# Two small sums of an attention and expert kernel: an operand laid out in strided pairs, and a ten-column product on another engine

## The chip, the cores and the metric

The kernel runs on one core of a Trainium2 chip. The core has five engines that each work off an instruction list of their own, in order: TensorE (PE in the tables; PEld is its weight load), VectorE (DVE), ScalarE (ACT), GpSimd (POOL) and SyncE (SP, which here only issues transfers). An instruction that has to wait for another engine holds up everything behind it on its own engine. The metric is the device time of one execution in microseconds (us).

## The reference, cut to what matters

Three layers follow one another, all in fp32: attention with 32 packing queries per head, a causal mixture of four expert heads with the two best gates per token, and a gated channel mix.

```python
def sm_attn(qq, kk, vv):                       # q, k, v: (8, 8, 576, 64), p: (8, 8, 32, 64)
    s = scale * qq @ kk.T
    a = exp(s - max(s))
    return a / (sum(a) + 1e-09) @ vv
p_packed = sm_attn(p, k, v)                    # 32 packed tokens per head
x = sm_attn(q, p_packed, p_packed)             # -> (8, 576, 512)

for e in range(4):                             # causal experts, head size 64
    a = exp(s_e - max(s_e))                    # s_e: masked scale * q_e @ k_e.T
    ye = a / (sum(a) + 1e-09) @ v_e @ wo[e]
    out += gate[e] * ye                        # gate: softmax over the two best, else 0

x_prev = out shifted by one token
k = relu((mu_k*x + (1-mu_k)*x_prev) @ w_k)
out = sigmoid((mu_r*x + (1-mu_r)*x_prev) @ w_r) * (k*k @ w_v)
```

The change touches the two places where `sum(a) + 1e-09` is formed: the one of the second attention step (`a / sum` over 32 packed tokens) and the one of the experts, where 1 / (sum + 1e-09) is multiplied by the gate.

## The kernel before, in words

Every fp32 product is made of reduced-precision matmuls on a high and a low part of each operand, so that much of the work beside TensorE is to split tiles: the high part is a cast (names that end in `h`), the low part a difference (names that end in `l`).

The program has two stages. In the first, up to about 465 us, the eight batches (b = 0 to 7) go through attention and experts. Their work is written as small generators: `front(b, g)` is the attention for group g of four heads, `values`, `project`, `soft` and `turn` are the experts' projections, masked exponentials and transposes, `pair_out(b, ep)` is the output of a pair of experts, and `fold` prepares products of weights for the second stage. Tables of hand-written times (`FRONT_T`, `G1_T`, `SOFT_T`, `OUT_LAG`, `FOLD_T`) sort the steps of all generators into one program order; a scheduler in the framework then works out each engine's list from a simulated time and priorities. On the chip the lists are fixed. In the second stage (`kstage` at line 855, `vstage` at line 888, up to 862 us) the channel mix runs as long rows of matmuls.

In `front`, each of the 16 instances (8 batches, 2 groups) holds a tile `st` of 128 partitions by 576 columns, read as 18 blocks of 32. Line 326 sums each block on DVE into `s` (128x18), line 327 adds the epsilon to `s` in place, line 329 takes the reciprocal into `r`, and line 330 multiplies `st` by `r`, on POOL for all batches but the first. Line 323, a little earlier, makes `PWl`, the low part of a PSUM tile. A PSUM tile of that size (`big`) is used in turns by many steps, so the next use waits until the tile is read out.

In `pair_out`, each of the 16 instances (8 batches, 2 pairs of experts) reads `sums`, 5 row tiles by 4 experts for each partition. A pair takes two of every four numbers, so the operand is five pairs at a stride of four; line 546 adds the epsilon and writes ten adjacent numbers `cs`, line 547 takes the reciprocal, line 548 multiplies by the gates `cw` (the tile `gws` in the trace). Then `cx`, a copy of the ten numbers to 640 columns, is made (line 206 on DVE in batches 0 to 6, line 204 on ACT in the last), which TensorE transposes later.

Other names below: line 488 makes the masked scores `ms` of one row tile and their minimum `nb` on DVE, line 492 is their exponential on ACT, line 428 the low parts `l` (of `qs`) and `kl` (of `ks`), which read a `big` tile out of PSUM. `A2h` and `A2l` are the two parts of the attention weights. On POOL, lines 687, 200 and 650 are steps of `fold` and of the splits: `wc` (times `om`), `wh` and `wl`.

Of the kernel before, what the change touches and what calls it, by code (L numbers as in the profile page):

```python
# [9 lines left out]
F32 = mybir.dt.float32  # L10
# [4 lines left out]
ALU = mybir.AluOpType  # L15
AX = mybir.AxisListType
# [3 lines left out]
EPS = 1e-9  # L20
# [37 lines left out]
def kernel(  # L58
# [4 lines left out]
    nc = tc.nc  # L63
    P = 128
# [11 lines left out]
    NCB = S // NPK  # L76
# [17 lines left out]
    def nm(s):  # L94
        uid[0] += 1
        return f"{s}_{uid[0]}"

    def big():
        return psb.tile([P, 1024], F32, tag="big", name=nm("big"))

    def one():
        return pso.tile([P, 512], F32, tag="one", name=nm("one"))
# [32 lines left out]
    def pool(name, bufs, side):  # L135
        cm = tc.tile_pool(name=name, bufs=bufs, side=side, reuse_waits="tile")
        return cm, cm.__enter__()
# [6 lines left out]
    if True:  # L144
# [3 lines left out]
        sm_cm, sm = pool("sm", 4, "left")  # L148
# [53 lines left out]
        def evac(eng, o, x):  # L202
            if eng == "A":
                nc.scalar.copy(o, x)  # L204
            elif eng == "V":
                nc.vector.tensor_copy(o, x)
            else:
                pool_copy(o, x)

        def pool_tt(o, x, y, op):  # L210
            nc.gpsimd.tensor_tensor(o, x, y, op=op)  # L211

        def scores_pair(lhs, rhs):
            ps = big()
            for hf in range(2):
                for jj in range(2):
                    nc.tensor.matmul(
                        ps[64 * jj : 64 * jj + 64, 512 * hf : 512 * hf + SH],
                        lhs[:, 64 * jj : 64 * jj + 64],
                        rhs[:, jj, SH * hf : SH * hf + SH],  # L220
                        start=True, stop=True,
                    )
            return halves(ps)[:, :, :SH]
# [23 lines left out]
        def front(b, g):  # L247
# [33 lines left out]
            for c in range(NT):  # L281
# [10 lines left out]
                op0=ALU.mult, op1=ALU.mult,  # L292
# [7 lines left out]
            s2 = scores_pair(ppT, qT)  # L300
# [3 lines left out]
            st3 = st.rearrange("p (c n) -> p c n", n=NPK)  # L304
# [17 lines left out]
            nc.scalar.copy(bat["PWh"][:, g, :], ps[:, :NQK])  # L322
            nc.vector.tensor_sub(bat["PWl"][:, g, :], ps[:, :NQK], f32(bat["PWh"][:, g, :]))
            yield
            s_ = sm.tile([P, NCB], F32, tag="s2", name=nm("s2"))
            nc.vector.tensor_reduce(s_, st3, op=ALU.add, axis=AX.X)
            nc.vector.tensor_scalar(s_, s_, EPS, None, op0=ALU.add)
            r_ = sm.tile([P, NCB], F32, tag="r2", name=nm("r2"))
            nc.vector.reciprocal(r_, s_)
            small.tensor_tensor(st3, st3, r_.unsqueeze(2).to_broadcast([P, NCB, NPK]), op=ALU.mult)  # L330
            yield
            a2 = fr.tile([P, S], F32, tag="sa", name=nm("a2"), bufs=4)
# [106 lines left out]
        def rowap(base, stride, n, w):  # L439
            return bass.AP(  # L440
                tensor=base.tensor, offset=base.offset, ap=[base.ap[0], [stride, n], [1, w]]
            )
# [4 lines left out]
        def tslice(tb, j, q0, q1):  # L447
            return tb[:, TS * j + q0 : TS * j + q1]
# [90 lines left out]
        def pair_out(b, ep):  # L539

            bat = bats[b]
            vg, cw, sums = bat["vg"], bat["cw"], bat["sums"]
            tabs = [bat.pop(("tb", 2 * ep + ee)) for ee in range(2)]
            cs = sm.tile([P, NT, 2], F32, tag="cs", name=nm("cs"), bufs=2)
            es = slice(2 * ep, 2 * ep + 2)
            nc.vector.tensor_scalar(cs, sums[:, :, es], EPS, None, op0=ALU.add)
            nc.vector.reciprocal(cs, cs)
            nc.vector.tensor_mul(cs, cs, cw[:, :, es])
            cx = ex.tile([P, NT, 2, HD], F32, tag="cx", name=nm("cx"), bufs=1)
            evac(E_CX if b < B - 1 else E_CXL, cx, cs.unsqueeze(3).to_broadcast([P, NT, 2, HD]))  # L550
            avs = []
            for lo, hi in ((QB, S), (0, QB)):
                av = one()
                nj = (hi + P - 1) // P
                for j in range(nj):
                    qo = max(lo, j * P)
                    for ee in range(2):
                        nc.tensor.matmul(  # L558
                            av[64 * ee : 64 * ee + 64, qo - lo : hi - lo],
                            vg[:, j, HD * (2 * ep + ee) : HD * (2 * ep + ee + 1)],  # L560
                            tslice(tabs[ee], j, qo, hi),
                            start=j == 0, stop=j == nj - 1,
                        )
                avs.append((av[:, : hi - lo], lo, hi))
            yield
            cp = big()
            for t in range(NT):
                nc.tensor.transpose(
                    cp[:, t * P : (t + 1) * P], cx[:, t, :, :].rearrange("p e h -> p (e h)"), ident
                )  # L570
            cb = ex.tile([P, 1 + S], F32, tag="cb", name=nm("cb"), bufs=1)
            nc.gpsimd.memset(cb[:, :1], 0.0)
            evac(E_CB, cb[:, 1:], cp[:, TAIL : TAIL + S])
            for ps_, lo, hi in avs:
                nc.vector.tensor_mul(cb[:, 1 + lo : 1 + hi], ps_, cb[:, 1 + lo : 1 + hi])


            dt = ex.tile([P, NS, ST], F32, tag="dt", name=nm("dt"), bufs=1)

            def tokens(o):  # L580
                return rowap(cb[:, o : o + 1], RT, ST, 1).rearrange("p s x -> p (s x)")

            pool_tt(
                dt[:, 0:4:3, :],
                bass.AP(tensor=cb.tensor, offset=cb.offset, ap=[cb.ap[0], [1, 2], [RT, ST]]),
                bass.AP(tensor=cb.tensor, offset=cb[:, 2:].offset, ap=[cb.ap[0], [1, 2], [RT, ST]]),
                ALU.subtract,
            )
            pool_tt(dt[:, 1, :], tokens(1), tokens(2), ALU.add)
            pool_tt(dt[:, 2, :], tokens(2), tokens(1), ALU.subtract)  # L590
            yield
            nc.sync.dma_start(dscr[:, NS * ep : NS * ep + NS, ST * b : ST * b + ST], dt)
            yield
# [334 lines left out]
        for b in range(B):  # L928
            t0 = U * b
            for g in range(NG):  # L930
                add(
                    "front", front(b, g), [t0 + t + g * G1_T[i] for i, t in enumerate(FRONT_T)],
                    None if b else PR0 - 10 * g,
                )
            add("values", values(b), [t0 + t for t in VAL_T])
            for ep in range(2):
                add("project", project(b, ep), [t0 + t for t in PROJ_T[2 * ep : 2 * ep + 2]])
            for e in range(NE):
                for i, group in enumerate(GROUPS):
                    t = t0 + NT * e + SOFT_T[i]  # L940
                    add("soft", call(soft, b, e, group), [t])
                    add("turn", call(turn, b, e, group), [t + TURN_LAG[i]])
            for ep in range(NE // 2):
                add("out", pair_out(b, ep), [t0 + 2 * NT * (ep + 1) + t for t in OUT_LAG])
# [66 lines left out]
```

## Time and profile before

| what | us |
|---|---|
| median of three runs (lowest to highest) | 862.37 (861.75 to 862.72) |
| the profiled execution, from its first to its last instruction | 861.8 |
| PE busy | 809.3 (94%) |
| DVE busy | 580.0 (67%) |
| ACT busy | 390.4 (45%) |
| POOL busy | 387.8 (45%) |

The times are device times of whole runs without a profile. The profile is of one further execution, and its span leaves 0.57 us to the median of the runs; no execution time other than its span is given for it. Busy time does not count waiting inside an engine's queue, but an instruction that is held up after it has started counts as busy for as long as it is held.

### The profile page before, as it was taken

How to read it: one execution, taken by the hardware profiler on the slowest of the kernel's cores; microseconds unless marked ns; L12 is line 12 of the kernel's file. 1: busy time of each engine (PE TensorE's matmuls, PEld its weight loads, DVE VectorE, ACT ScalarE, POOL GpSimd, SP SyncE). 2: the span in 40 equal slices, each digit the busy share in tenths (PEclk: the TensorE clock that was granted, in tenths of full speed). 3: DMA queues.
4: the chain of work that ended last, by engine and by line, in shares of the span. 5: the costliest groups of instructions: out<-in, count | busy, mean ns of one | idle time of the engine just before them, and what ended most of it. 6: DMA issues, size and time to landing. Idle time of an engine off the chain costs nothing. (4 is left out here: it accounts for less than half of the span.)

```text
span 861.8 us, 14939 instructions
## 1 busy us (share of the span) xinstructions
PE 809.3 (94%) x5376; PEld 678.2 (79%) x5376; DVE 580.0 (67%) x1306; ACT 390.4 (45%) x989; POOL 387.8 (45%) x525
## 2 busy tenths in 40 slices
PE   6798999999799899988799998999999999999998
PEld 5485868779587696857667877988888889898896
DVE  3989796888958759899885775545454544544342
ACT  2367667686665767767566562202112122121120
POOL 4577577575765645446451242333413233232230
PEclk9799999999999999999999999999999999999999
DMA  9654553736335255425446984032121231120301
GB/s 312 228 164 154 144 173 112 230 110 165 127 116 161 76 150 162 136 79 161 122 158 219 344 294 170 2 121 74 49 110 37 86 111 49 74 74 4 144 1 74
DMA packets 67290, 113.71 MB, mean 132 GB/s; under 512 B 10128, under 2 KB 46480, under 8 KB 67216
## 3 DMA queue, kind: packets, MB, share of 16 engines
q1 hardware_dynamic: 66640, 112.69, 40.6%
q8 instruction: 43, 0.70, 0.3%
q14 instruction: 31, 0.25, 0.1%
q10 hardware_dynamic: 576, 0.07, 0.1%
HBM read 69.74 MB, written 33.55 MB: 120 GB/s over the span
## 5 line engine op out<-in xcount | busy, mean ns | idle before, releaser
L888 PE MATMUL one<-wvh,kk 128*128 128x512 f32 x576 | 186.1, 391 | 0.4 <-DVE rr L893 0.3
L211 POOL TENSOR_TENSOR kk<-y,kk 128x768 fp32r<-128x768 f32 x48 | 89.7, 1869 | 210.5 <-ACT kk L868 206.8
L888 PEld LDWEIGHTS one<-wvh,kk 128*128 128x128 f32 x576 | 107.8, 188 | 21.7 <-DVE rr L893 1.0
L888 PE MATMUL one<-wvl,kk 128*128 128x512 f32 x288 | 112.5, 391 | 0.0
L492 ACT ACTIVATE ms<-ms,nb 64x64 f32<-64x64 f32 (+4 forms) x160 | 89.5, 559 | 36.1 <-DVE nb L488 34.1
L868 ACT CAST kk<-y 128x768 fp32r<-128x768 f32 x48 | 40.1, 835 | 133.2 <-DVE y L866 96.1
L816 DVE TENSOR_TENSOR y<-big,p 128x256 f32<-128x256 f32 x48 | 20.3, 424 | 117.1 <-POOL kk L211 101.2
L863 ACT COPY p<-big 128x256 f32<-128x256 f32 x48 | 17.9, 372 | 126.4 <-PE big L855 92.2
L204 ACT COPY tb<-one 64x128 f32<-64x128 f32 (+5 forms) x208 | 64.5, 355 | 22.4 <-PE one L522 19.6
L558 PE MATMUL one<-tb,vg 128*64 128x320 f32 (+4 forms) x448 | 59.9, 372 | 5.2 <-DVE nb L488 3.9
L888 PEld LDWEIGHTS one<-wvl,kk 128*128 128x128 f32 x288 | 54.3, 188 | 9.7
L515 PE MATMUL one<-ident,ms 128*128 128x128 f32 x320 | 56.1, 285 | 4.7 <-ACT ms L492 2.2
L558 PEld LDWEIGHTS one<-tb,vg 128*64 128x64 f32 x448 | 37.5, 141 | 26.0 <-DVE nb L488 5.1
L488 DVE CUSTOM_DVE_ANT_0 ms<-one,mstrip 64x64 f32<-64x64 f32 (+3 forms) x128 | 51.5, 420 | 6.8 <-PE one L476 4.6
L515 PEld LDWEIGHTS one<-ident,ms 128*128 128x128 f32 x320 | 39.2, 144 | 15.3 <-issue 3.7
L630 POOL TENSOR_TENSOR dcx<-dcx,dcu 128x256 f32<-128x256 f32 x40 | 31.2, 781 | 43.6 <-DVE dcu L624 34.0
L893 DVE TENSOR_TENSOR rr<-one,rr 128x512 f32<-128x512 f32 x36 | 23.2, 685 | 40.7 <-PE one L888 40.6
L866 DVE SCALAR_TENSOR_TENSOR y<-y 128x768 f32<-128x768 f32 x48 | 47.9, 998 | 1.6
L476 PE MATMUL one<-ks,qs 128*128 128x64 f32 (+3 forms) x128 | 41.6, 350 | 5.8 <-DVE nb L488 2.5
L855 PE MATMUL big<-dh,wk0h 128*128 128x256 f32 x192 | 39.7, 284 | 4.2 <-DVE rr L818 3.8
L200 POOL TENSOR_SCALAR dh<-dl 128x2048 fp32r<-128x2048 f32 x10 | 19.4, 1936 | 48.1 <-DMA dl<-dscr 32.8
L211 POOL TENSOR_TENSOR dt<-cb 128x192 f32<-128x192 f32 (+1 forms) x48 | 32.1, 694 | 19.5 <-issue 16.0
(189 smaller groups left out, 2167.3 us busy)
## 6 DMA issues: line engine op xcount, KB each, us to landing
dl<-dscr SPq DMA_DIRECT2D x10, 1024.0 KB, 6.7
kT<-in_k_dram SPq DMA_DIRECT2D x16, 576.0 KB, 4.3
qT<-in_q_dram SPq DMA_DIRECT2D x16, 576.0 KB, 4.9
rscr<-rr SPq DMA_DIRECT2D x12, 768.0 KB, 4.0
rr<-rscr SPq DMA_DIRECT2D x12, 768.0 KB, 4.3
out_dram<-rr SPq DMA_DIRECT2D x11, 768.0 KB, 3.3
vn<-in_v_dram SPq DMA_DIRECT2D x16, 512.0 KB, 4.6
dscr<-dt SPq DMA_DIRECT2D x16, 384.0 KB, 3.8
```

The lines of the kernel that those rows point to most:

```text
L204: nc.scalar.copy(o, x)
L211: nc.gpsimd.tensor_tensor(o, x, y, op=op)
L476: nc.tensor.matmul(ps[:, po : po + kn], qs[:, i * P : i * P + P], keys[:, ko : ko + kn], start=x == 0, stop=x == 1,)
L488: nc.vector.tensor_tensor_reduce(halves(mv) if last else mv, sv, halves(mk) if last else mk, op0=ALU.add, op1=ALU.min, scale=-SC, scalar=3 ...
L492: nc.scalar.activation(mv, mv, AF.Exp, bias=nb[p0:], scale=-1.0, accum_out=bat["sums"][p0:, i, e : e + 1],)
L515: nc.tensor.transpose(ps[:, at + j * P : at + (j + 1) * P], ms[:, j * P : (j + 1) * P], ident)
L558: nc.tensor.matmul(av[64 * ee : 64 * ee + 64, qo - lo : hi - lo], vg[:, j, HD * (2 * ep + ee) : HD * (2 * ep + ee + 1)], tslice(tabs[ee], ...
L630: nc.gpsimd.tensor_add(f32(t["x"]), f32(t["x"]), f32(t["u"]))
L855: nc.tensor.matmul(ps[:, o : o + EB], wpart("k0" if f < 4 else "k1", s, wx, t)[:, f % 4 * P : f % 4 * P + P], dx[:, NS * t + s, :], start= ...
L866: nc.vector.scalar_tensor_tensor(y, y, 0.0, y, op0=ALU.max, op1=ALU.mult)
L868: nc.scalar.copy(kk[:, 0], y)
L888: nc.tensor.matmul(ps, kk[:, a, x, t0 : t0 + P], wres["v"][b][:, f, :], start=n == 0, stop=n == 3 * NFT - 1,)
```

## The change

In `front`, the 18 block sums are written to a tile of 9 by 4 numbers, of which the first two of each four are used. The epsilon is then added from this strided operand into the 18 adjacent numbers of `r`, and the reciprocal is taken in `r` in place. The sums' tile has two buffers in place of four, with as many bytes in all. In `pair_out`, the product of `cs` and the gates moves from DVE to POOL.

```diff
-            s_ = sm.tile([P, NCB], F32, tag="s2", name=nm("s2"))
-            nc.vector.tensor_reduce(s_, st3, op=ALU.add, axis=AX.X)
-            nc.vector.tensor_scalar(s_, s_, EPS, None, op0=ALU.add)
+            s_ = sm.tile([P, NCB // 2, 4], F32, tag="s2", name=nm("s2"), bufs=2)[:, :, :2]
+            nc.vector.tensor_reduce(
+                s_, st3.rearrange("p (a b) n -> p a b n", b=2), op=ALU.add, axis=AX.X
+            )
             r_ = sm.tile([P, NCB], F32, tag="r2", name=nm("r2"))
-            nc.vector.reciprocal(r_, s_)
+            nc.vector.tensor_scalar(r_.rearrange("p (a b) -> p a b", b=2), s_, EPS, None, op0=ALU.add)
+            nc.vector.reciprocal(r_, r_)
             small.tensor_tensor(st3, st3, r_.unsqueeze(2).to_broadcast([P, NCB, NPK]), op=ALU.mult)
...
             nc.vector.tensor_scalar(cs, sums[:, :, es], EPS, None, op0=ALU.add)
             nc.vector.reciprocal(cs, cs)
-            nc.vector.tensor_mul(cs, cs, cw[:, :, es])
+            nc.gpsimd.tensor_tensor(cs, cs, cw[:, :, es], op=ALU.mult)
```

All lines below the first hunk stand two lines lower in the changed kernel: its line 330 adds the epsilon, 331 is the reciprocal, 332 the product with `st`, and 548, 549 and 550 are the former 546, 547 and 548. Each engine's list also changes elsewhere. Three places show how. The number behind a name tells one tile from another of the same kind.

Place A is DVE's list in batch 3, where the first pair's `cs` (`cs_3269`) is due while masks of later row tiles are made (ISA is the masked minimum of line 488, now 490). Before:

```order
L488 ISA ms_122,nb_689_3245<-one_3240,mstrip 128x192
L488 ISA nb_689_3245 128x1
L488 ISA ms_123,nb_690_3248<-one_3240,mstrip 128x320
L488 ISA nb_690_3248 128x1
L548 TENSOR_TENSOR cs_3269<-cs_3269,gws_2813 128x10
L323 TENSOR_TENSOR PWl_2413<-big_3143,PWh_2412 128x772
L488 ISA ms_124,nb_692_3257<-big_3252,mstrip 128x576
L488 ISA nb_692_3257 128x1
L206 COPY cx_3273<-cs_3269 128x640
```

Now, the same place on DVE, from the reciprocal's successor on:

```order
L490 ISA ms_122,nb_689_3245<-one_3240,mstrip 128x192
L490 ISA nb_689_3245 128x1
L490 ISA ms_123,nb_690_3248<-one_3240,mstrip 128x320
L490 ISA nb_690_3248 128x1
L490 ISA ms_124,nb_692_3257<-big_3252,mstrip 128x576
L490 ISA nb_692_3257 128x1
L323 TENSOR_TENSOR PWl_2413<-big_3143,PWh_2412 128x772
L206 COPY tb_3047<-one_3265 64x64
L326 TENSOR_REDUCE s_673_3184<-st_3067 128x9x2
L262 TENSOR_REDUCE mx_700_3296<-big_3291 128x1
L330 TENSOR_SCALAR r_674_3186<-s_673_3184 128x18
L206 COPY cx_3273<-cs_3269 128x640
```

And POOL's list there, now with the product between two of its long operations:

```order
L718 TENSOR_TENSOR oo_2745<-oo_2745 128x256
L200 TENSOR_SCALAR A2h_2410<-a_681_3213 128x576
L550 TENSOR_TENSOR cs_3269<-cs_3269,gws_2813 128x10
L689 TENSOR_SCALAR wc_3101<-wc_3101,om 128x256 x4
L337 TENSOR_TENSOR A2l_2411<-a_681_3213,A2h_2410 128x576
L332 TENSOR_TENSOR st_3067<-st_3067,r_674_3186 128x576
```

DVE's product is gone from between the masks, the low part `PWl` has changed places with the mask of 576 columns, and the copy `cx` has moved back by three instructions that stand behind `PWl`.

Place B is the second pair of batch 4. On DVE before, the copy stood behind the low part `l`:

```order
L546 TENSOR_SCALAR cs_4480<-sums_3598 128x10
L547 RECIPROCAL cs_4480<-cs_4480 128x10
L548 TENSOR_TENSOR cs_4480<-cs_4480,gws_3568 128x10
L428 TENSOR_TENSOR l_4199<-big_4186,qs_118 128x576
L206 COPY cx_4484<-cs_4480 128x640
L428 TENSOR_TENSOR kl_120<-big_4213,ks_4226 64x576 x2
```

Now `l` stands ahead of the sums, and on DVE nothing lies between the reciprocal and the copy:

```order
L430 TENSOR_TENSOR l_4199<-big_4186,qs_118 128x576
L548 TENSOR_SCALAR cs_4480<-sums_3598 128x10
L549 RECIPROCAL cs_4480<-cs_4480 128x10
L206 COPY cx_4484<-cs_4480 128x640
L430 TENSOR_TENSOR kl_120<-big_4213,ks_4226 64x576 x2
```

On POOL the product now stands behind eight instructions that split weights and queries:

```order
L200 TENSOR_SCALAR qs_118<-qs_118 64x576
L200 TENSOR_SCALAR wh_3857<-wc_3856 128x256 x4
L652 TENSOR_TENSOR wl_3858<-wc_3856,wh_3857 128x256 x2
L461 MEMSET sums_5003 128x20
L550 TENSOR_TENSOR cs_4480<-cs_4480,gws_3568 128x10
L652 TENSOR_TENSOR wl_3858<-wc_3856,wh_3857 128x256 x2
```

The copy has to wait for the product, so it and `kl` behind it now hang on POOL's list.

Place C is the second pair of batch 2. On DVE before:

```order
L548 TENSOR_TENSOR cs_2970<-cs_2970,gws_2058 128x10
L206 COPY cx_2974<-cs_2970 128x640
L428 TENSOR_TENSOR l_2689<-big_2676,qs_118 128x576
L428 TENSOR_TENSOR kl_120<-big_2703,ks_2716 64x576 x2
L644 SCALAR_TENSOR_TENSOR wc_3101<-dcq_3109,dcx_3106 128x256
```

Now, with two steps of `fold` (`wc`, `dcx`) ahead of `kl`:

```order
L549 RECIPROCAL cs_2970<-cs_2970 128x10
L430 TENSOR_TENSOR l_2689<-big_2676,qs_118 128x576
L646 SCALAR_TENSOR_TENSOR wc_3101<-dcq_3109,dcx_3106 128x256
L206 COPY cx_2974<-cs_2970 128x640
L620 SCALAR_TENSOR_TENSOR dcx_3152<-raw_3150,dce_3153 128x256
L430 TENSOR_TENSOR kl_120<-big_2703,ks_2716 64x576 x2
```

On POOL the product stands behind all four `wl`:

```order
L200 TENSOR_SCALAR wh_2348<-wc_2347 128x256 x4
L652 TENSOR_TENSOR wl_2349<-wc_2347,wh_2348 128x256 x3
L461 MEMSET sums_3598 128x20
L652 TENSOR_TENSOR wl_2349<-wc_2347,wh_2348 128x256
L550 TENSOR_TENSOR cs_2970<-cs_2970,gws_2058 128x10
```

The copy has moved from the place right behind the product to one behind `l` and `wc`, and `kl` from the next place but one to one behind `dcx`.

## Rows read from the trace of the kernel before

**Rows 1.** Windows: stretch, length, busy PE PEld DVE ACT POOL, PEclk, DMA share, GB/s.

```profile
0.00:470.00 470.00, 426.00 (x3142) 339.97 (x3144) 384.28 (x1037) 302.85 (x863) 273.35 (x463) 0.96 0.51 156
530.00:862.00 332.00, 327.69 (x1950) 291.79 (x1948) 155.48 (x228) 55.78 (x93) 96.82 (x52) 1.00 0.19 68
```

**Rows 2.** Instructions of tile cs: min/median/max ns, first and last start us.

```profile
L546 DVE TENSOR_SCALAR cs<-sums x16: 151/164/167, 74.2 to 458.1; 128x10 f32<-128x10 f32 x16
L548 DVE TENSOR_TENSOR cs<-cs,gws x16: 157/240/3573, 79.4 to 458.6; 128x10 f32<-128x10 f32 x16
L206 DVE COPY cx<-cs x14: 476/492/968, 81.7 to 404.7; 128x640 f32<-128x640 f32 x14
L204 ACT COPY cx<-cs x2: 709/718/726, 435.4 to 461.2; 128x640 f32<-128x640 f32 x2
```

**Rows 3.** Instructions of line 327, the epsilon of the block sums.

```profile
L327 DVE TENSOR_SCALAR s<-s x16: 134/386/2346, 25.5 to 389.2; 128x18 f32<-128x18 f32 x16
```

**Rows 4.** Timeline of DVE from 229 us: start, duration, instruction, [idle before <-releaser].

```profile
229.47 3.57 DVE L548 TENSOR_TENSOR cs<-cs,gws 128x10 f32<-128x10 f32 x1
232.96 0.95 DVE L323 TENSOR_TENSOR PWl<-big,PWh 128x772 fp32r<-128x772 f32 x1
```

**Rows 5.** Timeline of POOL over the same stretch.

```profile
229.14 0.95 POOL L687 TENSOR_SCALAR wc<-wc,om 128x256 f32<-128x256 f32 x2
...
231.60 1.41 POOL L335 TENSOR_TENSOR A2l<-a,A2h 128x576 fp32r<-128x576 f32 x1
```

**Rows 6.** Timeline of PE behind it.

```profile
234.06 1.40 PE L217 MATMUL big<-kT,pT 128*64 128x288 f32 x6 [3.47 <-DVE PWl L323]
```

**Rows 7.** Timeline of DVE from 284 us.

```profile
284.50 3.39 DVE L548 TENSOR_TENSOR cs<-cs,gws 128x10 f32<-128x10 f32 x1
287.81 0.74 DVE L488 CUSTOM_DVE_ANT_0 ms<-big,mstrip 128x576 f32<-128x576 f32 x1
```

**Rows 8.** Timeline of PE there.

```profile
288.62 0.87 PE L217 MATMUL big<-kT,pT 128*64 128x288 f32 x4 [2.69 <-DVE nb L488]
```

**Rows 9.** Windows around and behind the two waits, columns as in rows 1.

```profile
225.00:245.00 20.00, 16.29 (x105) 11.25 (x106) 14.92 (x36) 13.51 (x40) 13.09 (x23) 0.91 0.19 63
280.00:300.00 20.00, 17.31 (x116) 11.55 (x115) 14.76 (x36) 14.09 (x42) 13.69 (x23) 0.91 0.25 81
290.00:292.00 2.00, 2.00 (x9) 1.23 (x9) 1.51 (x4) 0.26 (x1) 0.00 (x0) 0.50 0.04 6
```

**Rows 10.** Timeline of DVE in batch 0's first pair.

```profile
74.98 0.66 DVE L327 TENSOR_SCALAR s<-s 128x18 f32<-128x18 f32 x1
```

**Rows 11.** Timeline of PE there.

```profile
76.70 1.54 PE L217 MATMUL big<-kT,pT 128*64 128x288 f32 x8 [0.83 <-DVE nb L488]
```

**Rows 12.** Instructions of line 330, the same product on both engines.

```profile
L330 POOL TENSOR_TENSOR st<-st,r x14: 1152/1161/1186, 72.9 to 392.3; 128x576 f32<-128x576 f32 x14
L330 DVE TENSOR_TENSOR st<-st,r x2: 759/872/986, 26.1 to 36.1; 128x576 f32<-128x576 f32 x2
```

**Rows 13.** Timeline of DVE in batch 4's second pair.

```profile
305.02 0.22 DVE L547 RECIPROCAL cs<-cs 128x10 f32<-128x10 f32 x1
...
308.46 1.52 DVE L428 TENSOR_TENSOR kl<-big,ks 64x576 fp32r<-64x576 f32 x2 [1.40 <-ACT ks L426]
```

**Rows 14.** Timeline of POOL there.

```profile
307.71 2.81 POOL L650 TENSOR_TENSOR wl<-wc,wh 128x256 fp32r<-128x256 f32 x4
```

**Rows 15.** Timeline of PE there.

```profile
310.83 0.42 PE L413 MATMUL big<-A2h,PWh 128*128 128x288 f32 x2
```

**Rows 16.** Timeline of DVE in batch 2's second pair.

```profile
197.75 1.52 DVE L428 TENSOR_TENSOR kl<-big,ks 64x576 fp32r<-64x576 f32 x2 [0.94 <-ACT ks L426]
...
199.77 0.78 DVE L618 SCALAR_TENSOR_TENSOR dcx<-raw,dce 128x256 int32<-128x256 int32 x1
```

**Rows 17.** Timeline of POOL there.

```profile
197.07 1.44 POOL L650 TENSOR_TENSOR wl<-wc,wh 128x256 fp32r<-128x256 f32 x2
```

**Rows 18.** Timeline of PE there.

```profile
200.00 0.43 PE L413 MATMUL big<-A2h,PWh 128*128 128x288 f32 x2
```

## The prediction, made before the changed kernel had run

> **What bounds the kernel now.** I read the windows by stage first. In the second stage PE is busy for 327.69 of 332 us at the full granted clock; the change has no instruction there. In the first 470 us PE is busy for 426.00, so 44 us are PE's waits, and DVE is the next busiest engine with 384 us [rows 1]. A gain must come out of waits of PE for DVE in the first stage; time taken from DVE where PE does not wait is worth nothing.
>
> Next I read the groups of the two places. They hold one odd thing. Line 548, a product of ten columns, takes between 0.16 and 3.57 us; line 327, an addition on 18 columns, between 0.13 and 2.35. Line 546, an addition on the same ten columns whose operand lies in strided pairs, never leaves 0.151 to 0.167 [rows 2, 3]. The reader is to see the spread: so small an instruction is not busy for 3 us, it is held. The timelines of DVE and POOL show by what: at 229.47 the product starts while POOL runs its operations from 229.14 back to back, and it ends at 233.04, when the last of six, `A2l`, ends (231.60 + 1.41) [rows 4, 5]. To add up the held time of 32 instances would give no price. Last I read PE's timeline: which of the holds does PE wait for?
>
> Two large ones. After 230.59 PE waits 3.47 us, until `PWl` is there, which stands directly behind the product at 229.47 [rows 4, 6]. After 285.93 it waits 2.69 us for the mask behind the product at 284.50, which is held 3.39 us [rows 7, 8]. A smaller one: the addition at 74.98 is held for 0.66 us and the mask behind it ends a PE wait of 0.83 [rows 10, 11]. I take the other holds as covered: behind no other long one did I find a wait of PE that it ended.
>
> **What each wait costs.** The two large ones cost more than themselves. [...] 20 x 0.09 = 1.8 us of full-speed work each, if all of it lay on PE's path. [...]
>
> **The change part by part.**
>
> *The product leaves DVE (16 times).* At place A, batch 3, DVE comes past the product's old place at 229.55. Now the 576-column mask (0.74, and 0.08 to read its minimum) and then `PWl` (0.95) follow [rows 4, 7]: 229.55 + 0.82 + 0.95 = 231.3. `PWl` was ready at 233.91 before (232.96 + 0.95), PE's matmul began 0.15 behind it, so it begins at about 231.45 in place of 234.06: 2.6 gained. In batch 4 the mask follows the reciprocal directly, so it ends at 284.50 + 0.82 = 285.3, ahead of 285.93, where PE runs out of work: I take the whole 2.7. With the clock's 2 x 1.8 = 3.6 that is 8.9.
>
> *The addition in strided pairs (16 times).* If the form is what spares line 546, line 327's median of 0.39 goes to about 0.16. On the path stands only batch 0's: 0.66 - 0.16 = 0.5. If the form does nothing this is 0. The block sum writes 9x2 numbers in place of 18; no row of before shows that form, and I take no difference: the count of numbers is the same, and at 0.2 us each way in 16 places off the path it would still be nothing. Two buffers for four: the tile is read once, right behind its writing, in the same list, so nothing waits for it.
>
> Full gain: 2.6 + 2.7 + 3.6 + 0.5 = 9.4.
>
> *The product arrives on POOL.* POOL took 1.16 us for a product of 576 columns where DVE takes 0.76 to 0.99 [rows 12]. No row shows ten columns there. It is not below the 0.16 that DVE needs at least [rows 2] and not above 1.16; I take 0.3, nearer to the lower end, as ten columns are a sixtieth of 576. [...]
>
> *What queues behind it.* The price is POOL's list. The copy `cx` on DVE now waits for a product that stands in its turn on POOL, and everything behind the copy on DVE waits too. In the first pairs of batches 3 and 4 the copy stands behind `PWl` and the masks, so POOL has time. In the second pairs it does not.
> - Place B, batch 4. Before, POOL had done `wh`, `qs` and a memset by 307.71 and then four `wl`, 0.70 each (2.81) [rows 14]. Now two of them stand ahead: 307.71 + 1.40 + 0.3 = 309.4, which is 4.2 us after the reciprocal (305.02 + 0.22) [rows 13]. The copy takes 0.49 [rows 2], `kl` 1.52: 311.4. Before, `kl` ended at 309.98 and PE read the next tile of that kind at 310.83 [rows 13, 15]: 0.85 of slack, so 0.6 late.
> - Place C, batch 2. The four `wl` end at 198.51 [rows 17], the product at 198.8, the copy at 199.3, then `dcx` 0.78 and `kl` 1.52: 201.6, against 199.27 before and PE's next use at 200.00 [rows 16, 18]: 1.6 late, or 0.8 if `dcx` is not ready in time to matter.
> I take 0.6 + 1.2 = 1.8 of new waits. In the last batch ACT makes the copies, the last at 461.2, 2.6 behind the last product [rows 2]; that time covers the move.
>
> **The sum.** I keep half of the clock's 3.6, since PE will still stand still near these places for a while and the new waits may bring falls of their own: 9.4 - 1.8 - 1.8 = 5.8. The profiled execution's span is 861.8, 0.57 below the median of the runs, and I make the sum on the median: 862.4 - 5.8 = 856.6. The bounds of the terms: all of the gain and no new wait, 853.0; no clock back and the product at 1.16 in both second pairs (0.9 more each), 862.4 - 9.4 + 3.6 + 1.8 + 1.8 = 860.2.
>
> **The rivals.**
> - *Only one of the large waits goes.* For it: in batch 4 I know that the mask is early, but not that PE's next operand is; every list has changed. Then 2.7 + 1.8 of the gain is lost: 9.4 - 4.5 - 1.8 = 3.1, so 859.3.
> - *Nothing changes.* The hold is not the product's alone: any instruction of DVE that contends with POOL's burst is held in its place, and the copy `cx` is one that varies (0.476 to 0.968 [rows 2]). If the copy, behind the product on POOL, meets the next burst, the wait moves and 862.4 stands, within 1.7. Against it: the copy's worst was half a microsecond. [...]
> - *Slower: DVE waits for POOL in the second pairs.* Each second pair has the product 4 us or so behind its reciprocal where POOL is in a split of weights, and DVE, in order, stands still. If three such places cost PE what the largest wait cost before, 3.4 us each and 1.8 for the clock, the price is 15.6 and the time 862.4 - 9.4 + 15.6 = 868.6. It decides from 9.4 us of new waits on. Against it: batches 2 and 4, worked out above, come to 0.6 and 1.6.
> - *The strided form does not help.* Both large waits hang on the product, so the time would be 857.1, inside the forecast's own range.
>
> **How the numbers follow.** 0.2% of the time, 1.7 us, is about what a measurement of this kernel can tell from no change. Forecast 0.55 (its own range 853 to 860.2); one wait only 0.15 (859.3, part of it within the bound: 0.02); nothing changes 0.17, of which 0.03 falls on faster and 0.02 on slower; slower 0.13 with a mild form (864 to 866) as likely as the full one. Faster: 0.55 + 0.13 + 0.03 = 0.71; same: 0.02 + 0.12 = 0.14; slower: 0.02 + 0.13 = 0.15. A range of 852.5 to 863.5 leaves out about 0.05 below and 0.13 above.
>
> **What would show it right or wrong.** On DVE no addition of the block sums above 0.2 us; if their spread stays, the form is not the reason that line 546 is free. No PE wait of 2 us or more for `PWl` in batch 3 and for a mask in batch 4, and the windows' clock there above 0.91. The ten-column product on POOL at about 0.3. New: DVE idle ahead of the copy `cx` with POOL as releaser, some 4 us in the second pairs of batches 2 and 4, and PE waits of 0.5 to 1.6 us for `kl` there. The forecast is wrong if these waits of DVE are as long in most batches and PE waits behind them, or if PE's waits in batches 3 and 4 stay with another releaser.

## The result and the profile after

The changed kernel takes 849.06 us (847.99 to 850.12, 4 runs) against 862.55 us (861.75 to 863.12, 4 runs) of the kernel before on the same chip: a ratio of 0.9847, with a 95% interval of 0.9831 to 0.9864. It is 13.5 us faster; 5.8 were forecast, and the time lies below the range of 852.5 to 863.5. The profiled execution has a span of 848.0 us, 13.8 below that of before.

The windows by stage of the changed kernel, columns as in [rows 1], and the stretches around the two places of [rows 9]:

```profile
0.00:470.00 470.00, 434.07 (x3216) 346.57 (x3217) 378.32 (x1030) 308.13 (x869) 280.25 (x483) 0.99 0.54 164
225.00:245.00 20.00, 19.78 (x144) 15.05 (x144) 15.10 (x45) 16.49 (x51) 17.00 (x31) 1.00 0.35 98
280.00:300.00 20.00, 18.84 (x152) 16.22 (x149) 10.42 (x30) 14.82 (x44) 13.35 (x26) 1.00 0.41 119
```

In the same 470 us PE is busy 8 us longer, and the trace has 74 matmuls more. At both places the granted clock is now 1.00 over the 20 us, where it had a mean of 0.91.

The instructions of tile `cs` and of the new line 330 (the block sums' epsilon), min/median/max in ns:

```profile
L548 DVE TENSOR_SCALAR cs<-sums x16: 121/164/167, 73.3 to 446.1; 128x10 f32<-128x10 f32 x16
L550 POOL TENSOR_TENSOR cs<-cs,gws x16: 196/210/386, 75.9 to 447.0; 128x10 f32<-128x10 f32 x16
L206 DVE COPY cx<-cs x14: 429/846/3667, 78.8 to 395.5; 128x640 f32<-128x640 f32 x14
```
```profile
L330 DVE TENSOR_SCALAR r<-s x16: 127/160/172, 24.4 to 379.2; 128x18 f32<-128x18 f32 x16
```

The epsilon's additions have lost their spread ([rows 3]: up to 2346 ns; now 172), and the product on POOL takes 0.21 us (median of 16). The holds have not all gone: the copy `cx` took at most 0.97 us before [rows 2] and takes up to 3.67 now. The timelines of batch 3's first pair (DVE, POOL, PE) show why that costs nothing there, where the copy takes 2.13 us:

```profile
228.77 0.75 DVE L490 CUSTOM_DVE_ANT_0 ms<-big,mstrip 128x576 f32<-128x576 f32 x1
229.50 0.96 DVE L323 TENSOR_TENSOR PWl<-big,PWh 128x772 fp32r<-128x772 f32 x1
...
232.29 2.13 DVE L206 COPY cx<-cs 128x640 f32<-128x640 f32 x1
```
```profile
230.67 0.20 POOL L550 TENSOR_TENSOR cs<-cs,gws 128x10 f32<-128x10 f32 x1
```
```profile
229.18 0.75 PE L560 MATMUL one<-tb,vg 128*64 128x320 f32 x2
229.59 1.31 PE L217 MATMUL big<-kT,pT 128*64 128x288 f32 x8
```

The mask and `PWl`, on which PE had waited 3.47 us [rows 6], come ahead of the copy; PE goes through without a wait, and the 2.13 us hold falls where PE has other work. Behind the longest hold, the 3.67 us in batch 2, PE waits 0.42 us for the instruction that follows the copy on DVE:

```profile
185.31 0.76 PE L570 MATMUL big<-ident,cx 128*128 128x128 f32 x5 [0.42 <-DVE su L268]
```

The new wait of DVE at place B, the second pair of batch 4, is there, but half as long as forecast (rows of DVE, POOL, PE):

```profile
296.55 0.22 DVE L549 RECIPROCAL cs<-cs 128x10 f32<-128x10 f32 x1
299.01 1.01 DVE L206 COPY cx<-cs 128x640 f32<-128x640 f32 x1 [2.24 <-POOL cs L550]
300.25 1.52 DVE L430 TENSOR_TENSOR kl<-big,ks 64x576 fp32r<-64x576 f32 x2 [0.23 <-ACT ks L428]
```
```profile
298.76 0.22 POOL L550 TENSOR_TENSOR cs<-cs,gws 128x10 f32<-128x10 f32 x1
```
```profile
302.78 0.42 PE L415 MATMUL big<-A2h,PWh 128*128 128x288 f32 x2
```

`kl` ends at 301.77, 1.0 us ahead of PE's next use of such a tile: no PE wait.

To see where the 13.8 us arise I use the first additions of `cs` as marks, since each kernel has them: the first pair of batch 3 (mark 1, at 228.51 before), the first pair of batch 5 (mark 2, 337.62) and the last pair of all (mark 3, 458.11). The table has the difference to before in each stretch, in us, from the profiled executions; it takes in the experiments below. The last column is the median time over before's on the same chip.

| kernel | to mark 1 | 1 to 2 | 2 to 3 | 3 to end | span | ratio |
|---|---|---|---|---|---|---|
| changed | -0.7 | -9.2 | -2.1 | -1.8 | 848.0 | 0.985 |
| changed, again | -0.1 | -9.1 | -1.4 | -3.1 | 848.2 | 0.986 |
| epsilon only | +0.3 | -3.9 | -1.1 | -1.9 | 855.1 | 0.997 |
| product only | -0.9 | -6.1 | -0.5 | -2.6 | 851.6 | 0.993 |
| two places only | -0.7 | -9.4 | +0.9 | -1.9 | 850.7 | 0.991 |
| all but two places | -0.5 | +3.5 | +2.3 | -1.1 | 866.0 | 1.008 |
| first six batches | -1.4 | -9.0 | -0.4 | -1.3 | 849.7 | 0.988 |
| last two batches | +0.8 | -0.3 | -1.6 | -2.3 | 858.5 | 0.997 |

So 9.2 us come from batches 3 and 4, and some 4 from behind mark 2. Of the last stretch's 1.8 us, 0.8 lie in the second stage, where no run changes the program: from the first matmul of line 855 (another number in the other kernels) to the end the profile of before takes 342.7 us, and all the others 341.9 to 342.2. Every run of the table gains 1 to 3 us in the last stretch, also those that keep before's lists there. So this part hangs to some extent on the one profile of before.

PE's waits between marks 1 and 2 add up to 7.3 us before and to 1.4 in the changed kernel. Of the 9.2 us, 5.9 are thus waits; the 3.3 that are left are for the two falls of the clock, 1.7 each. This is an estimate, and I make it in the same way further on.

### The profile page after: what moved, and what is told of

Its sections match the earlier page's. It is cut to its first block, busy times and chain, and to the rows that moved or that the text cites. A ratio compares the mean times of both kernels' runs of the same rounds, so it can differ in the third digit from the quotient of the medians.

```text
span 848.0 us, 14936 instructions
## 1 busy us (share of the span) xinstructions
PE 803.5 (95%) x5376; PEld 673.3 (79%) x5376; DVE 566.2 (67%) x1290; ACT 389.8 (46%) x989; POOL 391.1 (46%) x541
## 5 line engine op out<-in xcount | busy, mean ns | idle before, releaser
L560 PE MATMUL one<-tb,vg 128*64 128x320 f32 (+4 forms) x448 | 62.2, 367 | 7.2 <-ACT tb L204 4.8
L517 PE MATMUL one<-ident,ms 128*128 128x128 f32 x320 | 54.1, 279 | 4.4 <-ACT ms L494 1.7
```

Source lines behind the costliest of these rows:

```text
L517: nc.tensor.transpose(ps[:, at + j * P : at + (j + 1) * P], ms[:, j * P : (j + 1) * P], ident)
L560: nc.tensor.matmul(av[64 * ee : 64 * ee + 64, qo - lo : hi - lo], vg[:, j, HD * (2 * ep + ee) : HD * (2 * ep + ee + 1)], tslice(tabs[ee], ...
```

## Experiments

My theory A was: the product's hold in the first pairs of batches 3 and 4, with the clock that falls behind the PE waits, is worth some 9 us; the rest comes from a new order late in stage one. The rivals are named with each run.

**One edit alone.** The first run keeps `nc.vector.tensor_mul(cs, cs, cw[:, :, es])` and takes over the strided sums; the second does the reverse.

> Only the strided pairs of the block sums; the ten-column product stays on DVE. Theory A (the product's hold in the first pairs of batches 3 and 4 is the gain, some 9 us with the clock, and the rest comes from a new order late in stage one): the holds of the product stay, 860.5 to 863.5 us, the epsilon's addition never above 0.2 us. Rival B (the two edits share the gain, since the epsilon's additions held DVE for 8 us in all): 855 to 858.

> Only the product on POOL; the block sums' epsilon stays as it was. Theory A: 849 to 854.5 us (9 us from batches 3 and 4, and up to 4 more if the new order late in stage one comes with this part). Rival B: 856 to 859, and long holds of the epsilon's addition with PE waiting behind them.

The strided sums alone: 857.62 us, ratio 0.9966 (0.9939 to 0.9993). The product alone: 853.54 us, ratio 0.9929 (0.9901 to 0.9956). The first is below what theory A expected, and in the range of rival B, by which the epsilon's own holds have a share; the second is as theory A expected and below rival B's range. The trace of the first, PE's rows with a wait at the two places, then its clock there:

```profile
235.32 0.55 PE L517 MATMUL one<-ident,ms 128*128 128x128 f32 x3 [2.93 <-DVE tb L206]
...
286.68 1.19 PE L217 MATMUL big<-kT,pT 128*64 128x288 f32 x8 [2.67 <-DVE nb L490]
```
```profile
225.00:245.00 20.00, 17.07 (x128) 13.01 (x127) 16.48 (x43) 14.60 (x44) 15.04 (x25) 1.00 0.26 82
280.00:300.00 20.00, 17.25 (x128) 12.40 (x127) 14.82 (x40) 15.18 (x46) 11.82 (x20) 1.00 0.26 78
```

The reader is to see that both long waits are still there (the product is held 3.86 and 3.37 us), and that the clock did not fall behind either. Between marks 1 and 2 this kernel gains 3.9 us, and PE's waits there are only 0.6 shorter (6.7 against 7.3). So in this profile most of the gain is that of two falls that did not take place, 1.7 us each by this estimate, not that of the epsilon's additions. What decides on a fall is not shown. The order of the instructions around the wait does not decide it alone: at batch 4's place PE, ACT and POOL have the lists of before, and so has DVE but for the epsilon's new form, and the wait is as long (2.67 against 2.69), but only before's profile has a fall. This is one execution of each, and the ten runs of this kernel spread from 854.83 to 864.06 us, so that others may have the falls. The two parts alone gain 0.34% and 0.71%, together 1.5%: the intervals leave open whether they simply add. In the second run's trace both long waits are gone, but PE stands still for 2.0 of the 4 us from 306 on, which is a part of why it gains 6.1 us between the marks and not 9.2.

**The two places alone, and all but these.** The product's engine is chosen by place, in the kernel before and in the changed one:

```diff
-            nc.vector.tensor_mul(cs, cs, cw[:, :, es])
+            (nc.gpsimd if ep == 0 and b in (3, 4) else nc.vector).tensor_tensor(cs, cs, cw[:, :, es], op=ALU.mult)
```
```diff
-            nc.gpsimd.tensor_tensor(cs, cs, cw[:, :, es], op=ALU.mult)
+            (nc.vector if ep == 0 and b in (3, 4) else nc.gpsimd).tensor_tensor(cs, cs, cw[:, :, es], op=ALU.mult)
```

> The kernel before with the product on POOL in the first pairs of batches 3 and 4 alone, 2 of 16 places. Theory A: 853 to 855 us, with no PE wait of 2 us at 230 and 286 and a full clock behind them. Rival C (the gain is spread over all places, or is one of order): 2 of 16 of 13.5 us, so 860.5 to 862.

> The changed kernel with the product back on DVE in the first pairs of batches 3 and 4 alone. Theory A: 849.1 + 9 = 857 to 859 us, with the two long PE waits back. Rival C: 849 to 851.

Two of 16 places take the time to 852.54 us, ratio 0.9912 (0.9885 to 0.9938); its trace has no PE wait at 230, one of 1.34 us for ACT at 280, and a clock of 1.00 at both places. That the gain is spread over all places, one half of rival C, falls. The other half, that it is one of order, does not fall yet, since the lists of batches 3 and 4 are new here as well; outside these batches they are those of before. All but these two: 866.92 us, ratio 1.0076 (1.0049 to 1.0102), slower than before and 8 us slower than theory A expected. DVE's product there, and PE's rows with a wait:

```profile
228.90 5.15 DVE L550 TENSOR_TENSOR cs<-cs,gws 128x10 f32<-128x10 f32 x1
```
```profile
234.77 0.75 PE L217 MATMUL big<-kT,pT 128*64 128x288 f32 x2 [4.72 <-DVE nb L490]
...
290.16 0.71 PE L217 MATMUL big<-kT,pT 128*64 128x288 f32 x4 [3.13 <-DVE nb L490]
...
418.05 0.30 PE L478 MATMUL one<-ks,qs 128*128 128x64 f32 x1 [4.71 <-DMA ks<-ks]
```

The same small product is held for 5.15 us, to 234.05, and POOL's run there ends at 234.01: the hold is 1.58 us longer than the 3.57 of before, at another place in POOL's list. PE's waits at the two places, 4.72 and 3.13 us, are longer than the 3.47 and 2.69 of before. Late in the stage this order also waits 4.71 us for the transfer of `ks`; the like wait of the changed kernel is 1.36. So a new order can also lose there.

**A hold put back in an unchanged order.** The runs above move other instructions too. Here the changed kernel gets one more DVE instruction in each of the two places, whose result nobody reads. In the first two runs no other instruction changes place, in the third only a few beside it:

```diff
+            if ep == 0 and b in (3, 4):
+                junk = sm.tile([P, NT, 2], F32, tag="junk", name=nm("junk"), bufs=1)
+                nc.vector.tensor_mul(junk, sums[:, :, es], cw[:, :, es])            # first run
+                nc.vector.tensor_scalar(junk, sums[:, :, es], EPS, None, op0=ALU.add)  # second run
+                nc.vector.tensor_scalar(junk, cs, EPS, None, op0=ALU.add)           # third run
```

> The changed kernel, with one more instruction on DVE in the first pairs of batches 3 and 4, right behind the addition of the epsilon: a ten-column product of two SBUF operands (sums times gates) into a tile that nobody reads. All other instructions stand in the order of the changed kernel. Theory A (such a product is held through POOL's burst, and PE waits for the masks behind it): both are held for 1 us or more, PE waits of over 1 us come back at both places, and the time is 3 to 9 us above the changed kernel's 849, with a lower clock behind the waits. Rival C (the gain came from the new order alone): within 1.7 us of 849.

> The same as the run before with the added instruction in another form: the addition of a constant to the ten strided pairs, into the same unread tile. Theory A: 0.15 to 0.17 us each, never held, and the time within 1.7 us of 849. Rival D (any instruction more at these places moves PE's inputs and costs): the same time as with the product.

> The changed kernel with one more addition of a constant on DVE in the first pairs of batches 3 and 4, again into an unread tile, but from ten adjacent numbers to ten adjacent numbers. Against the run with the strided pairs it tells whether the layout alone decides on the hold. Theory A (the even, adjacent form is held like a product of two SBUF operands): held for 1 us or more at one place at least, a PE wait of over 1 us behind it at batch 3. Rival H (any operation of one operand is free): 0.15 to 0.2 us at both places, and no wait.

The added instruction in the three runs, in the same order:

```profile
L552 DVE TENSOR_TENSOR junk<-sums,gws x2: 1466/2144/2821, 226.8 to 280.3; 128x10 f32<-128x10 f32 x2
```
```profile
L552 DVE TENSOR_SCALAR junk<-sums x2: 152/153/154, 227.4 to 277.6; 128x10 f32<-128x10 f32 x2
```
```profile
L551 DVE TENSOR_SCALAR junk<-cs x2: 1823/2499/3175, 227.7 to 281.8; 128x10 f32<-128x10 f32 x2
```

Ten columns each time. In these places a product of two SBUF operands is held (2.82 and 1.47 us), an addition between two adjacent runs of ten numbers is held too (3.17 and 1.82), and the addition from strided pairs is not (0.15 at both). Between the two additions only the form differs: rival H falls. PE behind the first of each: the first run's row and its window there, then the third run's row:

```profile
230.39 0.75 PE L563 MATMUL one<-tb,vg 128*64 128x320 f32 x2 [2.28 <-DVE nb L490]
```
```profile
225.00:245.00 20.00, 17.54 (x122) 12.45 (x119) 14.20 (x42) 14.06 (x44) 13.96 (x24) 0.91 0.24 64
```
```profile
231.70 0.48 PE L563 MATMUL one<-tb,vg 128*64 128x320 f32 x1 [2.73 <-DVE nb L490]
```

The wait and the lower clock are back at batch 3, in the first run without any change of order. Between marks 1 and 2 the run with the product takes 3.4 us longer than the one with the strided pairs, the even addition 3.8. Times: 852.11 us, ratio 0.9890 (0.9875 to 0.9905), with the product; 850.89, ratio 0.9871 (0.9853 to 0.9888), with the pairs; 854.08, ratio 0.9913 (0.9882 to 0.9944), with the even addition, on the chip on which the changed kernel has 850.16. The even addition costs 3.9 us to the end, as at its place. The product costs 1.2 at the end, below the 3 to 9 that I expected, and the intervals overlap: at batch 4 it was held only 1.47 us, with a PE wait of 0.44, and later stretches gave some back. The holds are shorter here than the 3.57 and 3.39 of before because POOL's run is cut: POOL's own product, further on in its list, waits for the reciprocal that stands behind the held instruction on DVE. POOL's row in the first run, at batch 3:

```profile
229.78 0.21 POOL L553 TENSOR_TENSOR cs<-cs,gws 128x10 f32<-128x10 f32 x1 [0.23 <-DVE cs L549]
```

POOL is idle from 229.55 on, and the hold of 2.82 us ends at 229.57. In the kernel before, with the epsilon alone, with all but two places and in this run, all eight holds of the first pairs of batches 3 and 4 end within 0.05 us of the end of POOL's run. The clock's fall at batch 3 is worth 1.3 to 1.4 us here: the two runs take 3.4 and 3.8 us longer than the one with the strided pairs, and PE's waits are 2.0 and 2.5 longer. So the hold is shown at its place, where it costs 3.4 us and more, and order alone, the other half of rival C, falls too. That the longer holds of before are worth the whole 9.2 is not shown in this way; it rests on PE's waits there. The price at the end is clear with the even addition, each of whose runs is slower than each of the changed kernel's on that chip, and less so with the product.

**The copy on ACT.** One argument of the copy's call is changed, so that line 204 makes it in all batches:

```diff
-            evac(E_CX if b < B - 1 else E_CXL, cx, ...)
+            evac("A", cx, ...)
```

> The changed kernel with the copy cx on ACT in all batches. The copy on DVE was held up to 3.67 us in the changed kernel, with no PE wait behind it. Theory A (a hold costs only where PE waits behind it): within 2.5 us of 849, either way, from the new order alone. Rival E (the holds of the copy still cost some us, spread out): 842 to 846.

866.50 us, ratio 1.0055 (1.0034 to 1.0076): both expectations are wrong. The long holds of the copy are gone (0.71 to 0.77 us on ACT), but ACT has 14 copies more, and the lists are others. At mark 2 it is still 4.7 us ahead of before; then PE's longest wait of the stage:

```profile
414.14 0.39 PE L478 MATMUL one<-ks,qs 128*128 128x64 f32 x1 [6.53 <-DMA ks<-ks]
```

It says nothing on the copy's holds alone, since the order changed with it. It shows again the wait for `ks`, late in the stage, at which these orders differ most.

**The last batches.** The first run has the product back on DVE in the last batch, with all else in place. The next two make both edits by batch, `b < 6` or `b >= 6`: up to these batches the lists are those of the one kernel, behind them those of the other, save for some rows at the seam. The changed kernel itself ran beside them.

> The changed kernel with the product back on DVE in the last batch alone; nothing else changes its place. Theory A (what the changed kernel gains late in stage one does not come from a hold of the last batch's product, which took 0.17 us on DVE before): within 1 us of 849. Rival F (the gain of 4 us late in stage one is the product's there): 852 to 854.

> Both edits in batches 0 to 5 alone; the last two batches as in the kernel before. Theory A (10 us come from batches 3 and 4, and 3 to 4 us from the new order and the clock late in stage one): 851 to 854 us. Rival G (late in stage one the two kernels differ only from run to run): the same time as the changed kernel, 848 to 851.

> Both edits in batches 6 and 7 alone. Theory A: 3 to 4 us faster than before, 858 to 860 us, with the two long PE waits at 230 and 286 still there. Rival G: within 1.7 us of before.

> The changed kernel once more, beside the three others on the same chip. Expected 848 to 851 us; its late waits and falls of the clock, beside those of its first profile, show what varies from run to run.

The product on DVE in the last batch: 850.82 us, ratio 0.9869 (0.9849 to 0.9888). That is more than the 1 us above 849 that I had named, but the changed kernel did not run on this chip, and the run with the strided pairs, which did, has 850.89: no difference that can be told. First six batches: 852.04, ratio 0.9883 (0.9857 to 0.9909). Last two: 859.47, ratio 0.9970 (0.9956 to 0.9983), with the PE waits of 3.45 and 2.67 us at the two places still there. The changed kernel: 850.16, ratio 0.9862 (0.9839 to 0.9885). The gains of the two parts, 10.6 and 3.1, add up to 13.7, beside 12.4 for both. Theory A's split holds. The intervals of the first six and of the whole overlap, so that the last two batches' share is told best by their own run, whose interval of 1.5 to 3.8 us does not reach zero.

What this share is made of stays open. In the last pair of batch 7 the new list has a shorter wait of PE, 0.84 in place of 1.18 us. PE's rows of before, of the first six (before's list there) and of the last two (the new list):

```profile
455.52 0.33 PE L515 MATMUL one<-ident,ms 128*128 128x128 f32 x1 [1.18 <-ACT tb L204]
```
```profile
444.69 0.47 PE L524 MATMUL one<-ident,ms 128*128 128x128 f32 x1 [1.19 <-ACT tb L204]
```
```profile
452.51 0.33 PE L524 MATMUL one<-ident,ms 128*128 128x128 f32 x1 [0.84 <-ACT p L848]
```

From 440 to 470 us the mean clock is 0.94 in the first two, and 1.00 in the third and in both profiles of the changed kernel. That looks like one more fall that the new list avoids. But two other runs have before's list there, PE stands still there too, and there is no fall: 1.6 of the 4 us from 448 with the epsilon alone and 1.4 of the 4 us from 444 with the two places alone, beside 1.8 of the 4 us from 452 before. Their windows, in this order:

```profile
440.00:470.00 30.00, 28.28 (x151) 22.68 (x151) 20.10 (x35) 18.48 (x33) 8.71 (x11) 1.00 0.54 187
```
```profile
440.00:470.00 30.00, 28.25 (x151) 22.62 (x150) 18.80 (x32) 18.02 (x33) 7.11 (x7) 1.00 0.68 227
```

So the fall can stay away with before's list too, and it is not shown that the new list is what avoids it.

## Why the prediction was right or wrong

The mechanism of the main terms was right. The time came out below the range because three steps failed: the clock's term was halved, new waits were charged that did not come, and what lies behind mark 2 was no term.

**Right.** The bound (waits of PE for DVE in stage one), the two places and their releasers: with 2 of 16 products moved, the time falls by 9.1 us on that run's chip, beside 13.5 for the whole change. The terms of the full list for batches 3 and 4, 2.6 + 2.7 + 3.6 = 8.9, against 9.2 between marks 1 and 2, of which 5.9 are waits and 3.3 are left for the clock. That the sum comes so near is in part luck: the waits were 0.6 too low and the clock 0.3 too high. The strided pairs: no addition above 0.172 us, and of two additions on ten columns the added instructions took 0.15 us in the strided form and 1.82 and 3.17 in the even one. The product on POOL at 0.3: 0.21 measured.

**Not shown.** Batch 0's 0.5: to mark 1 the changed kernel gains 0.7 in the first profile and 0.1 in the second, and the run with the epsilon alone, which has this edit, loses 0.3.

**Wrong: "I keep half of the clock's 3.6".** There was no ground in a row for the half; the waits were gone and both falls with them. By the estimate above the term is 3.3, nearly the whole 3.6, so some 1.8 was missed here. No run shows the 1.8 for each fall; it was my estimate, the 20 us of [rows 9] times the 0.09 that their mean clock of 0.91 lacks. In its place the runs showed 1.7 each between marks 1 and 2 and 1.3 to 1.4 at batch 3 with the added instructions, by the lengths of the stretches less PE's waits. In the run with the epsilon alone both falls are gone (1.00) while the waits stay (2.93 and 2.67 us), so they are a term of their own.

**Wrong: "I take 0.6 + 1.2 = 1.8 of new waits".** PE has no wait at either place. At place B the eight POOL instructions stood there as forecast, but I timed the product by the old list's 307.71. In that list POOL's splits begin 0.2 us behind the reciprocal's start, in the new one 1.7 us ahead of it. The product ended 2.2 us behind the reciprocal's end, not 4.2, and `kl` was 1.0 ahead of PE. At place C the copy stood behind `l`, which waited 2.28 us for ACT's `qs`; the product was done 1.7 us before the copy began. So the step that failed is to put a new order on the old timeline without letting the other instructions move with it.

**Missing: what lies behind mark 2.** 2.1 us between marks 2 and 3 and 1.8 behind mark 3 were no term of the sum; the forecast looked at three places of an order that changed nearly everywhere. The new lists of the last two batches alone gain 3.1 us (1.5 to 3.8), so a part of it is theirs. The product's hold in the last batch is not the cause, as that batch's run and its 0.17 us on DVE before show. 0.8 of the 3.9 us lie in the second stage. The first six batches, with before's lists late in stage one, have 1.7 in their profile as well, the second stage included. What brings the gain about was not found: a shorter wait of 0.3 us is seen, and a fall of the clock that also stays away without the new lists.

1.8 + 1.8 + 3.9 = 7.5 of the 7.7 us that lie between 5.8 and 13.5: two terms of the wrong size, and a part that was no term and is hardly explained.

**The rivals.** "Nothing changes" was right that the copy would be held next (3.67 us), and wrong about the price: PE waited 0.42 us behind it. "Slower" was right that DVE would wait for POOL's product, 2.8 us in all before three copies, but PE paid nothing for the longest of these waits, at place B. "Only one wait goes" and "The strided form does not help" did not happen.

Held were the product (1.1 to 5.15 us), the even addition (1.82 and 3.17), the block sums' addition of before (up to 2.35 [rows 3]) and the copy: the one of 3.67 us at 181.58 ran beside five of POOL's instructions. Not held were the additions from five pairs into ten numbers (0.12 to 0.17 us) and from nine pairs into eighteen (0.13 to 0.17). Why POOL's run holds the one kind and not the other is not shown.

## What to carry to other kernels

A DVE instruction of ten columns was held here for up to 5.15 us while POOL went through a run of operations. Look for spread between the shortest and the longest instance of a small instruction (0.16 and 3.57 us for the product before), then for the one or two instances behind which PE waits. Here two of 16 products gave 9.1 of the 13.5 us, and behind their waits the granted clock fell as well (a mean of 0.91 over 20 us), some 1.7 us each by my estimate. What ended the holds here was to give a constant's addition an operand in strided pairs, five for ten columns and nine for eighteen (at most 0.17 us each), and to put the product into POOL's own list, where it took 0.20 to 0.39 us and made DVE wait up to 2.24 us for its turn. After that look at the whole order again: some 4 us came from behind the two places here, and the variant with the copy on ACT lost 5.6 us behind mark 2.

## What the runs showed of the hardware that was not expected

- Holds outlasted several instructions of the other engine: 5.15 us for ten columns, and 3.67 us for a copy whose shortest instance takes 0.43. In eight cases the hold ended where POOL's run had its first gap, within 0.05 us.
- A PE wait of 2.93 us and one of 2.67 us left the granted clock at 1.00 in one profile, and waits of 3.45 and 2.67 us were followed by a fall in another (a mean of 0.91 over 20 us), at the second place with the same instructions around it. One fall is worth 1.3 to 1.7 us, an estimate from the stretches' lengths less PE's waits.
- Between 400 and 440 us the mean clock is 1.00 in the first profile of the changed kernel and 0.91 in the second, with spans of 848.0 and 848.2; from 340 to 380 it is 0.96 in the first and 1.00 in the second. So falls lie at different places in two executions of one kernel.
